# Shorter pauses in batch 0's MLP chain, and the second pass begun with row 40 of the first, in a one-core attention and MLP backward kernel

## The chip, the cores and the metric

The kernel runs on one core of one Trainium2 chip. The metric is device time in microseconds (us) for one execution; lower is better. The kernel before takes 885.9 us, the median of three runs (885.33 to 886.79).

## What is computed

A decode-time transformer block (one query token, two batches), forward and backward. The forward part is a layer norm, attention of 32 heads over a cache of 4096 keys and values, an output projection with residual, then a second layer norm and a ReLU MLP with residual:

```python
def _A_ref(x, k_cache, v_cache, wq, wo):           # B=2, Sq=1, D=640, H=32, Sk=4096, Dh=128
    q = (x @ wq)...                                 # per head
    scores = einsum("bhqd,bhkd->bhqk", q, k) * Dh**-0.5
    p = softmax(scores)
    o = einsum("bhqk,bhkd->bhqd", p, v)
    return o... @ wo
h  = x + _A_ref(_layernorm(x), k_cache, v_cache, wq, wo)
h2 = h + relu(_layernorm(h) @ w1) @ w2              # Dff = 1728
```

The outputs are `h2` and, for a given `grad_out`, the gradients of `x`, both caches, `wq`, `wo`, `w1` and `w2`. The two cache gradients are as large as the caches: 64 heads in all (2 batches x 32), each with a K and a V tile of 1 MB to read and two tiles of 1 MB to write. Both are outer products: `gV[h] = p x go` and `gK[h] = ds x q`, where `go` (the gradient of the head's output) hangs on the whole forward pass of its batch and on the MLP's backward pass.

## The kernel before

**Two passes over 64 heads.** The first pass (`p1_iter`) has rows i = 0 to 65. Row i loads and transposes K of head i, forms its scores (`s_ps`), finishes the softmax of head i-1 (`nb` L533, `ep` L540, then the weighted keys `pk` in two halves at L486), and multiplies with V of head i-2 (`m_ps`, L476, and `u_ps`, L514). The second pass (`p2_iter`, index j = 0 to 64) makes the gradients: it reads V a second time as a W tile (not for the six last heads of each batch, whose V tiles are kept), forms `dp_ps`, and writes `gV` (j) and `gK` (j-1).

**Rows and steps.** Each row is recorded in eight steps, k = 0 to 7: the points at which `p1_iter` yields. The order of instructions on each engine is the order in which this Python code issues them (a manual schedule); every engine works its own list in order and waits at semaphores. Behind each step the outer loop (from L1244 on) pumps the load queue and lets background generators run for as much as a credit allows (`bg_step`, rates in `RATES`).

**Pauses.** A generator that has issued work for one engine and will next issue work for another that needs its result yields through `wait(n)`: it goes on n steps later, so that other instructions stand between the two in the engines' lists. `spread[0]` is 1 here, and 2 once the mixed stage has begun.

**The middle of batch 0.** When row 33 has been issued, `middle_gen(0)` starts. In row 34 it closes the attention output and calls `ln_fwd` (L232): `ssum` on DVE, a column sum on PE (`colsum`, L226), mean and variance, a second column sum, an inverse square root in a few tiny DVE operations (L257 to L282) that end in `x2c`. Then 70 `hf` matmuls (L799) on PE, the ReLU and its mask on DVE (L803 to L809), a pause, and fifteen DVE products against `w1` (L697, `ttr`), in three groups; each group needs a row `fbc` that PE spreads (`bcb_ps`, L661) and ACT copies (L663). `turn()` lets at most five such products into one row of this stretch, two in step 1 and one each in steps 3, 4 and 6. The backward layer norm and the products against `wo` of the first heads follow. Only when `go_group` has marked ("go", 0, 26) may j = 0 be issued.

**Which rows hold the second pass.** `P2_AT = H + 2 + M0_ITERS` is the first row with a j (H = 32). From there every second row has one; rows 64 and 65 both do, and from then on the second pass runs alone. Up to `P2_AT` the rows from 34 on leave six of the 32 columns of `pk` to ACT (L494); behind it only two rows do. Also in rows before `P2_AT` POOL copies the column and the probabilities (L502, L580), later ACT and DVE (L504, L580).

**Loads and stores.** A list `queue` is made ahead from the same plan: K of row i, V of row i-2, and a W tile one row ahead of its j. SP issues them in this order, each as soon as one of 13 buffers of 1 MB is free. Buffers come free when `pk`'s second half is done (K) or a row's last `m_ps` (V); six hold the kept V tiles of batch 0 until j = 5. In row `P2_AT - 1` one K buffer goes over to the gradients. In the mixed stage POOL issues the stores; in the second pass alone SP does.

Of the kernel before, what the change touches and what calls it, by code (L numbers as in the profile page):

```python
# [15 lines left out]
def kernel(  # L16
# [41 lines left out]
    def f_kc(c):  # L58
        return 128 if c < NFF else F_rem
# [92 lines left out]
    def wait(n):  # L152

        end = step[0] + n * spread[0]
        while step[0] < end and not forced[0]:
            yield 0.0
        yield
# [34 lines left out]
    x2c = cols.tile([128, ND, B], BF16)  # L192
    rstd2 = cols.tile([128, B], FP32)
# [29 lines left out]
    def colsum(src, n):  # L223

        t = pst([128, 16], FP32, "mid", "csum")
        nc.tensor.matmul(t[:, 0:n], lhsT=ones_f32, rhs=src, start=True, stop=True)  # L226
        return t

    def bc(ap, n):
        return ap[:, :, None].to_broadcast([128, ap.shape[1], n])  # L230

    def ln_fwd(xs, nb, xh, rstd):  # L232

        def st(name, dt=FP32):
            return small.tile([128, nb], dt, tag=f"ln_{name}{nb}", bufs=1, name=f"ln_{name}")
        ssum = st("ssum")
        nc.vector.reduce_sum(out=ssum[:], in_=xs, axis=AX.X)
        yield from wait(2)
        t1 = colsum(ssum[:], nb)
        yield  # L240
        mean = st("mean")
        nc.vector.tensor_scalar(out=mean[:], in0=t1[:, 0:nb], scalar1=1.0 / D, scalar2=None, op0=ALU.mult)
        cent = small.tile([128, nb, ND], FP32, tag=f"ln_cent{nb}", bufs=1, name="ln_cent")
        nc.vector.tensor_tensor(out=cent[:], in0=xs, in1=bc(mean[:], ND), op=ALU.subtract)
        sq = small.tile([128, nb, ND], FP32, tag=f"ln_sq{nb}", bufs=1, name="ln_sq")
        nc.vector.tensor_tensor(out=sq[:], in0=cent[:], in1=cent[:], op=ALU.mult)
        vs = st("vs")
        nc.vector.reduce_sum(out=vs[:], in_=sq[:], axis=AX.X)
        mean_bf = st("meanb", BF16)
        nc.vector.tensor_copy(out=mean_bf[:], in_=mean[:])  # L250
        y_bf = small.tile([128, nb, ND], BF16, tag=f"ln_y{nb}", bufs=1, name="ln_y")
        nc.vector.tensor_tensor(out=y_bf[:], in0=xs, in1=bc(mean_bf[:], ND), op=ALU.subtract)
        yield from wait(2)
        t2 = colsum(vs[:], nb)
        yield from wait(1)
        var_bf = st("varb", BF16)
        nc.vector.tensor_scalar(out=var_bf[:], in0=t2[:, 0:nb], scalar1=1.0 / D, scalar2=None, op0=ALU.mult)  # L257
        z_bf = st("zb", BF16)
        nc.vector.tensor_scalar(out=z_bf[:], in0=var_bf[:], scalar1=EPS, scalar2=None, op0=ALU.add)
        z = st("z")  # L260
        nc.vector.tensor_copy(out=z[:], in_=z_bf[:])
        y = st("r")
        yi = y[:].bitcast(mybir.dt.int32)
        nc.vector.tensor_scalar(out=yi, in0=z[:].bitcast(mybir.dt.int32), scalar1=1, scalar2=None,
                                op0=ALU.logical_shift_right)
        nc.vector.tensor_scalar(out=yi, in0=yi, scalar1=-1.0, scalar2=float(0x5f3759df), op0=ALU.mult, op1=ALU.add)
        yield from wait(1)
        while at_k[0] in (0, 7) and not forced[0]:
            yield 0.0
        t = st("t")  # L270
        for c3 in (-3.0, -12.0, -768.0):
            if nb == 1:
                nc.vector.scalar_tensor_tensor(out=t[:], in0=y[:], scalar=z[:, 0:1], in1=y[:],
                                               op0=ALU.mult, op1=ALU.mult)
            else:
                nc.vector.tensor_tensor(out=t[:], in0=y[:], in1=y[:], op=ALU.mult)
                nc.vector.tensor_tensor(out=t[:], in0=t[:], in1=z[:], op=ALU.mult)
            nc.vector.scalar_tensor_tensor(out=y[:], in0=t[:], scalar=c3, in1=y[:], op0=ALU.add, op1=ALU.mult)
        ba = st("ba", BF16)
        nc.vector.scalar_tensor_tensor(out=ba[:], in0=y[:], scalar=-1.0 / 8192, in1=z[:], op0=ALU.mult, op1=ALU.mult)  # L280
        nc.vector.reciprocal(out=rstd, in_=ba[:])
        nc.vector.tensor_tensor(out=xh.rearrange("p c b -> p b c"), in0=y_bf[:], in1=bc(rstd, ND), op=ALU.mult)  # L282
        yield from wait(3)

    def ln_bwd(gh, xh, rstd, add, dst, nb):

# [484 lines left out]
    def middle_gen(b):  # L771
        if o_next[0] < (b + 1) * H // OG:
            o_group()
        u4[0] = wide_row("u")[:, 0:256].bitcast(FP32)
        nc.vector.tensor_reduce(out=u4[0], in_=u_bank[0][:].rearrange("p (s d) -> p d s", s=4),
                                axis=AX.X, op=ALU.add)
        yield
        while a_next[0] < (b + 1) * H // OG:
            if a_next[0] == o_next[0]:
                o_group()  # L780
                yield
                yield
            a_group()
            yield
        at_bf = small.tile([128, ND], BF16, tag="at_bf", bufs=1, name="at_bf")
        nc.vector.tensor_copy(out=at_bf[:], in_=asum[:, b, :])
        nc.vector.tensor_tensor(out=h1c[:, :, b], in0=xg32[:, b, :], in1=at_bf[:], op=ALU.add)
        h32 = small.tile([128, 1, ND], FP32, tag="h32", bufs=1, name="h32")
        nc.vector.tensor_copy(out=h32[:, 0, :], in_=h1c[:, :, b])
        yield ("a", b)  # L790
        u_out(b)
        yield from ln_fwd(h32[:], 1, x2c[:, :, b:b + 1], rstd2[:, b:b + 1])
        wide = 32
        hf_w = pst([128, NF, wide], FP32, "mid", "hf_ps")
        hf_ps = hf_w[:, :, 0]
        for cf in range(NF):
            kc = f_kc(cf)
            for c in range(ND):
                nc.tensor.matmul(hf_w[0:kc, cf, :], lhsT=w1_t[:, c, cf * 128:cf * 128 + kc],  # L799
                                 rhs=x2c[:, c, b:b + 1].to_broadcast([128, wide]),  # L800
                                 start=(c == 0), stop=(c == ND - 1))
            yield 0.25
        nc.vector.tensor_scalar(out=acol[:, 0:NFF, b], in0=hf_ps[:, 0:NFF], scalar1=0.0, scalar2=None, op0=ALU.max)  # L803
        if F_rem:
            nc.vector.tensor_scalar(out=acol[0:F_rem, NFF, b:b + 1], in0=hf_ps[0:F_rem, NFF:NF],
                                    scalar1=0.0, scalar2=None, op0=ALU.max)
        mask = small.tile([128, NF], FP32, tag="mask", bufs=1, name="mask")
        nc.vector.tensor_single_scalar(out=mask[:], in_=acol[:, :, b], scalar=0.0, op=ALU.is_gt)
        nc.vector.tensor_tensor(out=ghfc[:, :, b], in0=ga[:, b, :], in1=mask[:], op=ALU.mult)  # L809
        yield from wait(3)  # L810
        fbc = wide_row("fbc")
        gx2 = small.tile([128, 1, ND], FP32, tag="gx2", bufs=1, name="gx2")
        gx2p = small.tile([128, ND, 3], FP32, tag="gx2p", bufs=1, name="gx2p")
        first_f = 0
        for k, n in enumerate((ND, ND, NF - 2 * ND)):
            row = fbc[:, (k % 2) * D:(k % 2 + 1) * D]
            w = spread_some(one(ghfc, b), k * ND, n, f_kc, row)
            yield
            for c in range(ND):
                yield from turn()  # L820
                part = w1_t[:, c, first_f:first_f + w]
                ttr(part, row[:, 0:w], gx2p[:, c, k:k + 1], w, part if b else later_heads())
                yield 0.85
            first_f += w
        nc.vector.reduce_sum(out=gx2[:, 0, :], in_=gx2p[:], axis=AX.X)
        yield ("w1", b)
        yield from ln_bwd(gx2[:], x2c[:, :, b:b + 1], rstd2[:, b:b + 1], gc[:, :, b:b + 1], gh1c[:, :, b:b + 1], 1)
        row = wide_row("hbc")
        hbc, junk = row[:, 0:D], row[:, D:2 * D]
        spread_some(one(gh1c, b), 0, ND, lambda c: 128, hbc)  # L830
        yield
        yield ("gh1", b)

        first = H - KEPT[b]
        bounds = [(first, first + 2), (first + 2, H)] if b == 0 else [(first, H)]
        bounds += [(h, min(first, h + GH)) for h in range(0, first, GH)]
        for h0, h1 in bounds:
            yield from go_group(b, h0, h1, hbc, junk)
        if b > 0:
            yield from mlp_out()  # L840
# [335 lines left out]
        forced[0] = False  # L1176

    EARLY = 2
    M0_ITERS = 7
    P2_AT = H + 2 + M0_ITERS  # L1180
    RATES = (0.2, 0.8, 0.2, 0.8, 0.45)
    RATE2 = 0.65
# [180 lines left out]
```

## Time and profile before

| what | value |
|---|---|
| median of three timed runs | 885.9 us |
| the profiled execution | 883.67 us, of which the profile's span is 881.9 us |
| mean granted TensorE clock | 0.784 |
| busy share PE, DVE, ACT, POOL | 83%, 77%, 56%, 20% |
| HBM | 211.11 MB read, 149.13 MB written, 408 GB/s over the span |
| loads K, V, W | 64, 64 and 52 of 1024 KB, 15 to 19 us from issue to landing |
| first pass alone (rows 0 to 40) | up to about 252 us |
| both passes (rows 41 to 65) | about 252 to 460 us |
| second pass alone, weight gradients, end | about 460 to 882 us |

The profile is of one execution. Its page cuts the span into 40 slices of 22 us and gives for each the busy share of the engines in tenths, the granted clock, the share of time that the 16 DMA engines were busy, and the GB/s they moved. Other views cut out any stretch, or list an engine's instructions in order of time with their start, duration and, in brackets, the idle time ahead of them and what ended it. A matmul's end is modelled, so starts are the better guide on PE.

### The profile page before, as it was taken

To read this page: it belongs to the slowest core of one execution; us is meant where nothing else is said; L and a number is where in the kernel's file an instruction comes from. 1 tells how busy PE (TensorE), PEld (TensorE's weight loads), DVE (VectorE), ACT (ScalarE), POOL (GpSimd) and SP (SyncE) were. 2 spreads that over 40 slices of the span, in tenths; PEclk is the share of its full clock that TensorE was granted. 3 is DMA by queue.
4 is the path that set the end of the run, shared out by engine and by line. 5 is a ranking of instruction groups with operands and counts; after the bars stand their busy time and mean duration, and the time that the engine had idled before them with its cause. 6 is when DMAs were issued, how large, how long until landed. Compare 5 with 4: busy or idle time off the path is not lost.

```text
span 881.9 us, 24851 instructions
## 1 busy us (share of the span) xinstructions
PE 730.4 (83%) x10143; PEld 609.8 (69%) x10143; DVE 680.9 (77%) x1281; ACT 497.9 (56%) x1292; POOL 172.7 (20%) x291
## 2 busy tenths in 40 slices
PE   4999989999998998987958677778867898957880
PEld 4888878888887887876848566656646666644550
DVE  2666978867888896966878898778787789889770
ACT  1344434445777664554536878777646766636560
POOL 1344433443311000000022100211001012201110
PEclk9999999999999999988985756556556756555555
DMA  9999999999989999999999999999999999999995
GB/s 379 425 419 422 417 416 412 422 417 422 369 302 415 424 423 425 423 424 425 408 396 396 409 426 426 424 425 425 424 425 421 424 424 422 426 425 425 424 422 231
DMA packets 56034, 361.86 MB, mean 410 GB/s; under 512 B 5680, under 2 KB 11504, under 8 KB 15216
## 3 DMA queue, kind: packets, MB, share of 16 engines
q1 hardware_dynamic: 46968, 303.29, 82.9%
q0 software_dynamic: 8912, 56.97, 15.6%
q8 instruction: 80, 1.31, 0.5%
q14 instruction: 34, 0.28, 0.1%
q10 hardware_dynamic: 40, 0.01, 0.0%
HBM read 211.11 MB, written 149.13 MB: 408 GB/s over the span
## 4 chain that ended last, share of the span: by engine, by line
PE 35%; DMA 34%; DVE 16%; ACT 8%; issue 4%; SPq 0%; DVEq 0%; POOL 0%; ACTq 0%; POOLq 0%
DMA Vt<-in_A_v_cache_dram 16%; PE t_ps L440 15%; DMA out_dram<-gV 9%; PE m_ps L476 8%; DMA out_dram<-gK 5%; DVE gK L866 4%; DVE gV L866 3%; DMA Wt<-in_A_v_cache_dram 3%; PE s_ps L453 3%; ACT t_sb L445 3%; ACT gV L956 3%; DVE pk L486 2%; PE u_ps L514 2%; DVE gxj L697 2%; PE dp_ps L453 2%
## 5 line engine op out<-in xcount | busy, mean ns | idle before, releaser
L445 ACT COPY t_sb<-t_ps 128x512 f32<-128x512 f32 x479 | 273.5, 588 | 188.8 <-PE t_ps L440 185.2
L453 PEld LDWEIGHTS <-t_sb 128*128 128x128 bf16 x4096 | 177.0, 102 | 60.3 <-ACT t_sb L445 34.3
L440 PE MATMUL t_ps<-ident_f,Wt 128*128 128x128 f32 x832 | 195.0, 384 | 1.0 <-ACT t_sb L445 1.0
L476 PE MATMUL m_ps<-pk,Vt 128*128 128x129 bf16 x2048 | 171.2, 222 | 17.1 <-DMA Vt<-in_A_v_cache_dram 15.9
L486 DVE TENSOR_TENSOR pk<-Kt,ep 128x2048 bf16<-128x2048 bf16 (+1 forms) x128 | 152.7, 1193 | 42.1 <-ACT ep L540 26.2
L866 DVE TENSOR_TENSOR gK<-rb,gsp 128x2048 bf16<-128x2048 bf16 x128 | 153.0, 1224 | 22.2 <-DMA out_dram<-gV 19.3
L476 PEld LDWEIGHTS <-Vt 128*128 128x128 bf16 x2048 | 124.8, 99 | 47.8 <-issue 28.7
L440 PE MATMUL t_ps<-ident_f,Kt 128*128 128x128 f32 x1024 | 154.7, 284 | 3.5 <-DMA Kt<-in_A_k_cache_dram 3.1
L866 DVE TENSOR_TENSOR gV<-rb,pp 128x2048 bf16<-128x2048 bf16 (+1 forms) x128 | 143.2, 1144 | 17.7 <-DMA out_dram<-gV 12.2
L440 PEld LDWEIGHTS t_ps<-ident_f,Wt 128*128 128x128 f32 x832 | 135.8, 199 | 28.3 <-issue 20.9
L440 PEld LDWEIGHTS t_ps<-ident_f,Kt 128*128 128x128 f32 x1024 | 113.1, 144 | 6.0 <-ACT t_sb L445 2.3
L502 POOL COPY pk<-ep 128x16 bf16<-128x16 bf16 x80 | 83.5, 1045 | 155.2 <-ACT ep L540 75.3
L453 PE MATMUL dp_ps<-gom,t_sb 128*128 128x2 bf16 x2048 | 95.3, 168 | 22.1 <-ACT t_sb L445 21.6
L453 PE MATMUL s_ps<-qm,t_sb 128*128 128x2 bf16 x2048 | 87.3, 164 | 1.2 <-DVE t_sb L443 1.2
L1010 ACT CAST ot<-o_ps 128x512 bf16<-128x512 f32 (+3 forms) x152 | 67.3, 491 | 10.2 <-PE o_ps L1004 8.8
L604 ACT CAST MT<-m_ps 128x128 bf16<-128x128 f32 x64 | 17.0, 266 | 94.0 <-PE m_ps L476 93.9
L911 POOL COPY pp<-P_bf 128x64 bf16<-128x64 bf16 x64 | 37.1, 581 | 133.3 <-DVE gV L866 132.0
L909 ACT ACTIVATE rb<-dp_ps,rt 128x256 bf16<-128x256 f32 x64 | 30.3, 473 | 44.2 <-PE dp_ps L904 44.2
L697 DVE CUSTOM_DVE_ANT_0 hbc<-wo_t,hbc 128x640 bf16<-128x640 bf16 x64 | 52.9, 826 | 0.3
L697 DVE CUSTOM_DVE_ANT_0 gxj<-wqs,gqr 128x1024 bf16<-128x1024 bf16 x40 | 48.8, 1220 | 0.2
L956 ACT ACTIVATE gV<-rb,pa 128x128 bf16<-128x128 bf16 x152 | 46.5, 393 | 1.0 <-DMA Wt<-in_A_v_cache_dram 0.9
L1013 POOL DMA_DIRECT2D out_dram<-ot x19 | 11.0, 579 | 153.6 <-ACT ot L1010 101.1
(208 smaller groups left out, 733.4 us busy)
## 6 DMA issues: line engine op xcount, KB each, us to landing
Kt<-in_A_k_cache_dram SPq DMA_DIRECT2D x64, 1024.0 KB, 18.7
Vt<-in_A_v_cache_dram SPq DMA_DIRECT2D x64, 1024.0 KB, 15.5
Wt<-in_A_v_cache_dram SPq DMA_DIRECT2D x52, 1024.0 KB, 17.4
out_dram<-gK SPq DMA_DIRECT2D x48, 1024.0 KB, 17.8
out_dram<-gV SPq DMA_DIRECT2D x47, 1024.0 KB, 18.1
out_dram<-gV POOLq DMA_DIRECT2D x17, 1024.0 KB, 9.8
out_dram<-gK POOLq DMA_DIRECT2D x16, 1024.0 KB, 10.2
wq_t<-in_A_wq_dram SPq DMA_DIRECT2D x5, 1024.0 KB, 6.8
```

Source lines behind the costliest of these rows:

```text
L440: nc.tensor.transpose(t_ps[:, j, :], natf[:, 2 * cc:2 * cc + 2, :].rearrange("p c k -> p (c k)"), ident_f[:])
L445: nc.scalar.copy(out=t_sb[:], in_=t_ps[:])
L453: nc.tensor.matmul(dst[:, sc:sc + 2], lhsT=v[:, j, :, par], rhs=vecs[:, par, :], start=(par == 0), stop=(par == 1))
L476: nc.tensor.matmul(r["m"][:, 0:129], lhsT=r["V"][:, sc, :], rhs=r["pk"][sc // HALF][:, sc % HALF, 0:129], start=(sc == 0), stop=(sc == NSC ...
L486: nc.vector.tensor_tensor(out=p["pk"][k][:, 0:n, 0:128].rearrange("p s (a two) -> p s a two", two=2), in0=p["K"][:, sl, :].rearrange("p s ...
L502: nc.gpsimd.tensor_copy(out=col, in_=e)
L697: nc.vector.tensor_tensor_reduce(out=junk[0:kc, 0:width], in0=in0, in1=in1, scale=1.0, scalar=0.0, op0=ALU.mult, op1=ALU.add, accum_out=acc)
L866: nc.vector.tensor_tensor(out=pairs_view(dst[:, sl, :]), in0=row.rearrange("p (a two) -> p a two", two=2)[:, None, :, :].to_broadcast([128 ...
L909: nc.scalar.activation(out=rb[:], in_=bank[:, 128:384], func=ACT.Copy, scale=rt[:, b, h:h + 1])
L911: nc.gpsimd.tensor_copy(out=pp[:], in_=P_bf[:, b * H + h, :, None].to_broadcast([128, NSC, 2]))
L956: nc.scalar.activation(out=gV[:, NSC - act + k, :], in_=c["rb"][:, 0:128], func=ACT.Copy, scale=pa[:, k:k + 1])
L1010: nc.scalar.copy(out=ot[0:P, k, n0:n0 + nn], in_=o_ps[0:P, 0:nn])
```

## The change

Four pauses are cut for batch 0 alone (`less` is 1 - b, and the ReLU's pause depends on b), and `M0_ITERS` goes from 7 to 6, so `P2_AT` from 41 to 40. Nothing that is computed changes, nor any operation's shape.

```diff
-    def ln_fwd(xs, nb, xh, rstd):
+    def ln_fwd(xs, nb, xh, rstd, less=0):
...
         nc.vector.reduce_sum(out=ssum[:], in_=xs, axis=AX.X)
-        yield from wait(2)
+        yield from wait(2 - less)
         t1 = colsum(ssum[:], nb)
...
-        yield from wait(2)
+        yield from wait(2 - less)
         t2 = colsum(vs[:], nb)
...
         nc.vector.tensor_tensor(out=xh.rearrange("p c b -> p b c"), in0=y_bf[:], in1=bc(rstd, ND), op=ALU.mult)
-        yield from wait(3)
+        yield from wait(3 - less)
...
-        yield from ln_fwd(h32[:], 1, x2c[:, :, b:b + 1], rstd2[:, b:b + 1])
+        yield from ln_fwd(h32[:], 1, x2c[:, :, b:b + 1], rstd2[:, b:b + 1], 1 - b)
...
         nc.vector.tensor_tensor(out=ghfc[:, :, b], in0=ga[:, b, :], in1=mask[:], op=ALU.mult)
-        yield from wait(3)
+        yield from wait(3 if b else 1)
...
-    M0_ITERS = 7
+    M0_ITERS = 6
```

What it does to the order: the inverse square root moves from row 35, step 1, to row 34, step 6; the `hf` matmuls from row 35, steps 4 to 7, to row 35, steps 0 to 3; the first L697 product from row 36, step 3, to row 35, step 4; the mark of the first heads from row 40, step 5, to row 39, step 6. The second pass's j = 0 to 11 come one row earlier each, j = 12 and 13 stay in rows 64 and 65, and row 63 then has none. In the load order each of the first W tiles stands one row earlier.

## The prediction

> **What bounds the kernel now.** I read the page's 40 slices first. The DMA and GB/s rows are the ones to follow:
>
> ```profile
> DMA  9999999999989999999999999999999999999995
> GB/s 379 425 419 422 417 416 412 422 417 422 369 302 415 424 423 425 423 424 425 408 396 396 409 426 426 424 425 425 424 425 421 424 424 422 426 425 425 424 422 231
> ```
>
> Nearly everywhere the DMA engines are full at about 424 GB/s. The clear hole before the last slice is slices 11 and 12, 220 to 264 us. Next the busy time by stretch, cut around that hole and in the long mixed stage behind it (columns: us, busy of PE, PEld, DVE, ACT, POOL, granted clock, DMA share, GB/s):
>
> ```profile
> 220.00:230.00 10.00, 9.49 (x167) 8.58 (x167) 6.57 (x20) 6.99 (x20) 2.87 (x4) 1.00 0.90 364
> 250.00:260.00 10.00, 9.64 (x162) 8.68 (x160) 8.91 (x21) 6.36 (x19) 1.14 (x4) 1.00 0.60 239
> 300.00:350.00 50.00, 45.82 (x782) 40.40 (x780) 40.98 (x87) 29.25 (x79) 3.92 (x9) 0.97 1.01 424
> ```
>
> So the kernel is a row of bytes at 424 GB/s, plus holes. What a change in the hole is worth is how much DMA time the hole swallows, before against after. Rows of the first pass can be timed by their L533 reduction (`nb`). The one at 208.86 us is row 34's: the layer norm's first casts (L786), issued in step 1 of row 34, stand right behind it. From the time-ordered list of DVE:
>
> ```profile
> 208.86 0.29 DVE L533 TENSOR_REDUCE nb<-s_ps 128x1 f32<-128x128 f32 x1
> ...
> 213.72 0.15 DVE L257 TENSOR_SCALAR ln_varb<-csum 128x1 bf16<-128x1 f32 x1
> ...
> 214.60 0.29 DVE L533 TENSOR_REDUCE nb<-s_ps 128x1 f32<-128x128 f32 x1
> 214.81 0.21 DVE L273 SCALAR_TENSOR_TENSOR ln_t<-ln_r,ln_z 128x1 f32<-128x1 f32 x1
> ...
> 216.54 0.17 DVE L282 TENSOR_TENSOR x2c<-ln_y,rstd 128x5 bf16<-128x5 bf16 x1
> ...
> 222.40 0.29 DVE L533 TENSOR_REDUCE nb<-s_ps 128x1 f32<-128x128 f32 x1 [0.43 <-PE s_ps L531]
> ...
> 228.93 0.29 DVE L533 TENSOR_REDUCE nb<-s_ps 128x1 f32<-128x128 f32 x1
> ...
> 253.21 0.29 DVE L533 TENSOR_REDUCE nb<-s_ps 128x1 f32<-128x128 f32 x1
> ```
>
> The other four L533 are those of rows 35 (214.60), 36, 37 and 41. Rows 34 to 40 take 253.21 - 208.86 = 44.35 us, 6.3 us each. Their loads need less: one K and one V tile, 2 x 1024 KB = 2.10 MB, at 424 GB/s 4.95 us. Here compute sets the pace, and loads wait for buffers that compute frees. DMA stays full until 226 us on what was queued, then starves. Two engines take turns as the limit: PE while the `hf` matmuls run (rows 34 and 35), DVE from 226 us, where five L697 products (0.82 us each) stand in one row.
>
> **The change part by part.** The mixed stage runs j = 0 to 11 on every second row, then 12 and 13 on rows 64 and 65, in both versions. After the change j = 0 to 11 come one row earlier, and row 63 is without one. Bytes, instructions and the program behind row 65 are the same. So only two things count: when the second pass starts, and how much has been loaded by then. It starts after six compute-bound rows, not seven. The dropped row's 2.10 MB are loaded later, in the DMA-bound stage, for 4.95 us. Thus the span changes by (new start - 253.21) + 4.95, where a "start" is the `nb` of the row that holds j = 0. To break even the new start must be at 248.26. The shorter pauses must make that possible: all of batch 0's layer norm, `hf`, 15 products, backward norm and first score heads must now fit in six rows.
>
> *Rows 34 and 35.* In the changed program's instruction order the first 30 `hf` matmuls stand behind row 35's first eight transposes, ahead of L531; before, they stood late in row 35. PE has this, from its time-ordered list:
>
> ```profile
> 213.44 1.07 PE L440 MATMUL t_ps<-ident_f,Kt 128*128 128x128 f32 x8
> 214.34 0.22 PE L531 MATMUL s_ps<-neg_ident,rmax 128*128 128x128 bf16 x1
> ...
> 218.01 0.92 PE L799 MATMUL hf_ps<-x2c,w_t 128*128 128x32 bf16 x30
> ```
>
> PE would reach `hf` at 214.34, but it needs `x2c`. The two column sums move up by 1 us at most and find their inputs ready. The half product `pk` in row 34 still starts at 212.18 (a buffer frees then, L476), and ends at 213.3. Then come the five operations from L257 (213.72 to 214.60, 0.88 us), now ahead of `rmax`, then `rmax`, 0.1, then the nine from L273 to L282 (214.81 to 216.71, 1.90 us), now ahead of `nb`. So `x2c` is done at 213.3 + 0.9 + 0.1 + 1.9 = 216.3 (0.1 for rounding of overlaps). PE waits 216.3 - 214.3 = 2.0 us; behind it, in order, stand L531 and all of row 35. First term: 2.0. Its bounds: 0 (if `pk` and the small operations pack tighter and the sums come a full step early) to 2.4.
>
> Then `hf` takes 0.77 (30 matmuls, 218.01 to 218.78 before), L531 goes at 217.1 and `nb` at 217.3. The rest of the row cost PE 222.14 - 214.34 - 0.77 = 7.0 us before, and five `bcb` transposes join it (0.3): PE reaches row 36's L531 at about 224.2. That needs `rmax`, which on DVE now stands behind the first product and the second `pk` half. The first product waits for `fbc` on ACT, and ACT has the six L494 activations ahead of that copy, where before it had not:
>
> ```profile
> 224.53 0.70 ACT L663 COPY fbc<-bcb_ps 128x640 bf16<-128x640 bf16 x1
> ...
> 225.92 1.86 ACT L494 ACTIVATE pk<-Kt,pe 128x128 bf16<-128x128 bf16 x6
> ```
>
> Before, the last four transposes of a row ended 2.25 us behind L531 (214.34 to 216.59); with 35 `hf` matmuls among them (half of the 0.77 + 0.82 + 0.72 us that all 70 took) now at 217.1 + 2.25 + 1.15 = 220.5. Then on ACT the copy (0.59), the six (1.86) and `fbc` (0.70), less 0.2 of overlap: 223.4. On DVE the product (0.82), `pk` (1.23) and `rmax`: 225.6. PE waits 225.6 - 224.2 = 1.4. Bounds: 0 (if PE is itself that late) to 2.3. One more product stands ahead of `nb`, so row 36's `nb` comes at 226.5.
>
> *Rows 36 to 39.* They hold what rows 37 to 40 held, 253.21 - 228.93 = 24.28 us, and one product more (13 behind `nb`, not 12). It is a narrow one, 0.62, and DVE idled 0.88 in row 39, so I add 0.2; the bounds are 0 and 0.8. Row 40, the new start, comes at 226.5 + 24.3 + 0.2 = 251.0. The second pass begins 2.2 us earlier, where 4.95 are needed.
>
> *The start of the mixed stage* has its own hole: 0.60 at 250 to 260 us, because one K buffer goes over to the gradients and the next load waits. The same buffers change hands one row earlier; I cost it at nothing. The cover is that DMA is full afterwards; if the first pair's heads come late (they are ready in step 6 of the row ahead, before in step 5) up to 0.5 more is lost.
>
> *The end of the first pass* runs at 391 GB/s (440 to 450 us), with DMA still full. One gradient store of 1.05 MB leaves that crowd: 1.05/391 - 1.05/424 = 0.2 us won; five such stores would be 1.0, the upper bound of that gain. One more row copies its column on ACT (2 x 0.26) and its probabilities on DVE (0.17), no longer on POOL, and one row fewer has the six L494 (1.86): all of it in rows that DMA paces. On SP each W load moves past one K and V pair, the same bytes in another order.
>
> *Sum:* (251.0 - 253.21) + 4.95 - 0.2 = +2.5 us. The profiled span 881.9 becomes 884.4; the median of the timed runs, 885.9, lies 4.0 above that span, so 888.4.
>
> **The rivals.**
> 1. *The waits are covered* (faster). If neither wait opens, the dropped row gives back its whole length, row 36's 228.93 - 222.40 = 6.53, against 4.95: -1.6, with the end of the pass -1.8, 884.1. For it: DVE was idle for nearly 4 us between 218 and 226, so there is room. Against: the room lies behind `hf`, and `hf` now stands ahead of its own input.
> 2. *Only one of the two opens*, about 2 us less than forecast: 886.4. For it: the second wait hangs on ACT's order and on PE being early, both estimates.
> 3. *The clock falls* (slower still). PE waits twice within 10 us. After a long wait PE had this:
>
> ```profile
> 409.00:413.00 4.00, 1.73 (x25) 1.45 (x22) 3.72 (x9) 1.32 (x4) 0.77 (x2) 0.94 1.01 422
> 413.00:417.00 4.00, 1.22 (x11) 1.22 (x12) 0.00 (x0) 0.08 (x1) 0.00 (x0) 0.50 1.01 428
> ```
>
> A granted clock of 0.50. At half clock for one row of 5.3 us PE loses 2.7 us in a stretch that it paces: 891.1. Against: from 280 to 284 us PE was busy for 2.19 of 4 us and kept 1.00. The Trainium skill, "TensorE: Matmul & The Clock Gate", section "What's actually happening", lets the clock fall after an idle window of about 3.4 us. By that rule this rival has no price, since my waits are 2.0 and 1.4; the two stretches above agree with it.
> 4. *The change does nothing of what it says*: a forced wait for the first heads would put j = 0 back behind unfinished work. The changed order excludes it: `GQc` of heads 26 and 27 stands ahead of j = 0's first product on DVE. No chance.
>
> **How the numbers follow.** Forecast 888.4 with 0.50; covered 884.1 with 0.20; one wait 886.4 with 0.18; clock 891.1 with 0.12. About 0.2%, 1.8 us, is what a measurement of this kernel can tell from no change: 884.1 and 887.7 are the edges. The forecast's own range, 887.0 to 889.9, comes from the bounds of the two waits and of rows 36 to 39, not all at one end. Slower: nine tenths of the forecast and the clock, 0.57. Faster: six tenths of "covered", 0.12. Same: the rest, 0.31. The range 884.0 to 891.0 leaves out half of "covered" and of the clock, 0.16.
>
> **What would show it.** Right: PE idle of about 2 us ahead of the first L799, released by DVE L282; a second idle ahead of L531 in the next row, released by L592; the six-row stage lasting about 42 us from `nb` to `nb`, at any rate over 39.4 (44.35 - 4.95); the DMA share falling before 226 us. Each step is wrong if its wait is under 0.5 us. All of it is wrong if the stage lasts about 37.8 us, or if the mixed stage runs under DMA share 0.98, since then the 4.95 us are not owed.

## The result, and the profile after

The change makes the kernel slower: 888.82 us (median of 8 runs, 887.51 to 890.25) against 886.27 us (8 runs, 885.33 to 889.81), a ratio of 1.0027 with a 95% interval of 1.0015 to 1.0039, that is 1.3 to 3.5 us. The profiled execution took 888.75 us, its span is 886.9. That of before, 883.67, was below every one of its timed runs: the two spans differ by 5.0, the medians by 2.6. Below, stretches of the two traces are compared with each other; verdicts come from the timed runs.

From the page after, the two rows that were shown of before:

```profile
DMA  9999999999689999999999999999999999999995
GB/s 377 424 420 421 417 416 413 422 418 419 263 309 408 423 423 425 424 424 426 421 408 410 415 426 420 425 426 425 425 425 410 425 424 419 421 426 424 425 421 229
```

The hole is still there and has become deeper where it begins: 263 GB/s in slice 11, where before had 369. Nowhere else is there a new one. By stretch (columns as before: us, busy of PE, PEld, DVE, ACT, POOL, granted clock, DMA share, GB/s):

```profile
210.00:220.00 10.00, 6.46 (x119) 5.63 (x116) 5.25 (x24) 4.60 (x14) 2.05 (x3) 0.83 1.02 422
220.00:230.00 10.00, 8.50 (x147) 7.50 (x146) 4.74 (x13) 5.08 (x15) 1.33 (x4) 0.83 0.46 183
250.00:260.00 10.00, 9.75 (x168) 8.71 (x165) 9.75 (x25) 7.20 (x21) 1.63 (x4) 1.00 0.65 261
430.00:500.00 70.00, 56.57 (x843) 49.88 (x841) 56.78 (x114) 42.78 (x115) 12.39 (x29) 0.80 1.01 411
```

From 210 to 230 us all three compute engines stand still for a good part, at a clock of 0.83; half of the DMA time from 220 to 230 is lost (0.46, before 0.90). The last line shows the other side: 411 GB/s where the first pass ends, before 398:

```profile
430.00:500.00 70.00, 50.71 (x766) 44.91 (x763) 55.00 (x110) 42.26 (x112) 13.59 (x29) 0.79 1.00 398
```

What stands still, and for whom, is in PE's time-ordered list:

```profile
213.49 1.07 PE L440 MATMUL t_ps<-ident_f,Kt 128*128 128x128 f32 x8
218.10 0.98 PE L799 MATMUL hf_ps<-x2c,w_t 128*128 128x32 bf16 x30 [3.54 <-DMA w_t<-in_B_w_dram]
218.92 0.27 PE L531 MATMUL s_ps<-neg_ident,rmax 128*128 128x128 bf16 x1
...
226.23 1.07 PE L440 MATMUL t_ps<-ident_f,Kt 128*128 128x128 f32 x8
228.80 0.23 PE L531 MATMUL s_ps<-neg_ident,rmax 128*128 128x128 bf16 x1 [1.50 <-DVE rmax L592]
```

and in DVE's:

```profile
216.06 0.17 DVE L282 TENSOR_TENSOR x2c<-ln_y,rstd 128x5 bf16<-128x5 bf16 x1
219.23 0.29 DVE L533 TENSOR_REDUCE nb<-s_ps 128x1 f32<-128x128 f32 x1 [3.00 <-PE s_ps L531]
...
226.67 0.82 DVE L697 CUSTOM_DVE_ANT_0 P_bf<-w_t,fbc 128x640 bf16<-128x640 bf16 x1 [2.09 <-ACT fbc L663]
...
228.56 0.19 DVE L592 TENSOR_REDUCE rmax<-s_ps 128x1 bf16<-128x32 f32 x1
...
229.40 0.28 DVE L533 TENSOR_REDUCE nb<-s_ps 128x1 f32<-128x128 f32 x1
...
254.43 0.29 DVE L533 TENSOR_REDUCE nb<-s_ps 128x1 f32<-128x128 f32 x1
```

Both waits are there. The second is as forecast: 1.50 us ahead of row 36's L531, whose `rmax` stands behind the first product and behind `fbc`. The first is longer (3.54 us, not 2.0) and has another cause: `x2c` was done at 216.23, as forecast (216.3), but the `hf` matmuls also need `w1`, and its load landed at 218.1. Row 36's `nb` is at 229.40 (forecast 226.5), the new start at 254.43 (forecast 251.0): the second pass, begun a row earlier, starts 1.2 us later than before. Rows 34 to 39 took 254.43 - 208.80 = 45.6 us, more than the seven rows before (44.35).

### The profile page after: what moved, and what is told of

It is laid out like the page before. It is cut to its first block, busy times and chain, and to the rows that moved or that the text cites. A ratio compares the mean times of both kernels' runs of the same rounds, so it can differ in the third digit from the quotient of the medians.

```text
span 886.9 us, 24838 instructions
## 1 busy us (share of the span) xinstructions
PE 741.0 (84%) x10143; PEld 618.5 (70%) x10143; DVE 680.7 (77%) x1282; ACT 496.9 (56%) x1288; POOL 167.4 (19%) x287
## 4 chain that ended last, share of the span: by engine, by line
DMA 35%; PE 33%; DVE 17%; ACT 7%; issue 4%; SPq 0%; DVEq 0%; ACTq 0%; POOL 0%; POOLq 0%
PE t_ps L440 14%; DMA Vt<-in_A_v_cache_dram 12%; DMA out_dram<-gV 12%; PE m_ps L476 8%; DVE gK L866 5%; DMA out_dram<-gK 4%; DVE pk L486 3%; DVE gV L866 3%; DMA Wt<-in_A_v_cache_dram 3%; PE s_ps L453 3%; ACT gV L956 3%; DMA w_t<-in_B_w_dram 2%; PE u_ps L514 2%; ACT t_sb L445 2%; PE dp_ps L453 2%
## 5 line engine op out<-in xcount | busy, mean ns | idle before, releaser
L453 PEld LDWEIGHTS <-t_sb 128*128 128x128 bf16 x4096 | 179.2, 103 | 60.4 <-ACT t_sb L445 33.0
L440 PE MATMUL t_ps<-ident_f,Wt 128*128 128x128 f32 x832 | 197.6, 387 | 0.9 <-ACT t_sb L445 0.9
L440 PEld LDWEIGHTS t_ps<-ident_f,Wt 128*128 128x128 f32 x832 | 137.8, 201 | 28.7 <-issue 21.6
L911 POOL COPY pp<-P_bf 128x64 bf16<-128x64 bf16 x64 | 33.9, 533 | 130.9 <-DVE gV L866 128.5
L697 DVE CUSTOM_DVE_ANT_0 hbc<-wo_t,hbc 128x640 bf16<-128x640 bf16 x64 | 53.0, 828 | 0.7 <-ACT hbc L663 0.4
L697 DVE CUSTOM_DVE_ANT_0 gxj<-wqs,gqr 128x1024 bf16<-128x1024 bf16 x40 | 48.8, 1221 | 0.2
L440 PE MATMUL t_ps<-ident_f,Vt 128*128 128x128 f32 x192 | 40.9, 354 | 1.6 <-ACT t_sb L445 1.6
```

What stands on the lines that cost most here:

```text
L440: nc.tensor.transpose(t_ps[:, j, :], natf[:, 2 * cc:2 * cc + 2, :].rearrange("p c k -> p (c k)"), ident_f[:])
L453: nc.tensor.matmul(dst[:, sc:sc + 2], lhsT=v[:, j, :, par], rhs=vecs[:, par, :], start=(par == 0), stop=(par == 1))
L697: nc.vector.tensor_tensor_reduce(out=junk[0:kc, 0:width], in0=in0, in1=in1, scale=1.0, scalar=0.0, op0=ALU.mult, op1=ALU.add, accum_out=acc)
L911: nc.gpsimd.tensor_copy(out=pp[:], in_=P_bf[:, b * H + h, :, None].to_broadcast([128, NSC, 2]))
```

## The experiments

All are timed against the kernel before on the same chip. "Start" is the L533 of the row with j = 0; before, 253.21. "Waits" are PE's idle times in the trace that another engine or a load ended, from row 34's L533 to the start: 0.8 us before, 6.0 in the changed kernel. Each trace is of one execution; before, e4 and e9, which are the same up to row 41, have their starts within 0.12 us of each other (253.21, 253.31, 253.19).

**Is it the landing of `w1`?** The load is queued two rows sooner, once in the changed kernel (e1) and once in the kernel before (e2):

```diff
-    W_AT = (14, 19, 25, 30, 35)
+    W_AT = (14, 19, 25, 30, 33)
```

> The changed kernel with the w1 load queued at row 33, not 35. Theory (PE's first wait is for the w1 load, which the earlier hf matmuls now meet): hf starts when x2c is done, near 216.2 and not 218.1; the wait ahead of it falls from 3.5 to about 1.7 us, the clock stays at 1.00, row 36's L531 comes 2 to 3.5 us sooner, the new start (L533 of row 40) near 251 and not 254.4, and the time falls by 2 to 3.4 us, to 885.4 to 886.8. Rival (the waits of rows 34 and 35 are hidden by full DMA queues and do not reach the end): 888.8 within 1.

> The kernel before with the w1 load queued at row 33. Theory (there hf stands so late that w1 has just landed): no change, 886.3 within 1. Rival (w1's landing paced row 35 before, too): faster by 1 us or more.

Measured: e1 892.62, ratio 1.0060 (1.0039 to 1.0082); e2 891.87, ratio 1.0045 (1.0025 to 1.0064). Both expectations failed on the time. PE's list of e1 shows why:

```profile
210.75 1.94 PE L440 MATMUL t_ps<-ident_f,Kt 128*128 128x128 f32 x8 [3.42 <-DMA Kt<-in_A_k_cache_dram]
...
223.37 0.90 PE L799 MATMUL hf_ps<-x2c,w_t 128*128 128x32 bf16 x30 [1.34 <-DVE x2c L282]
```

The local part was right: with `w1` there, `hf` waits 1.34 us for `x2c` alone. But the 2160 KB now go ahead of a K tile while DMA is full, and PE waits 3.42 us for that tile in row 34 (3.41 in e2). The granted clock then fell to 0.50, against e1's expectation that it would stay at 1.00: for 10.2 us in e1 (209.9 to 220.1) and 6.8 in e2. The second pass starts 3.6 us later than in the changed kernel in e1, and 5.5 us later than before in e2. With `w1` at row 35's place, in the kernel before, PE waits only 0.5 us for a load behind it (a V tile, at 222.87). So the load can't simply be moved: two rows sooner it delays other tiles, and the shorter pauses ask for it before it has landed. One row sooner was not tried.

**Which part of the change costs?** The pauses alone, second pass from row 41 (e3), then the ReLU's pause alone (e5) and the layer norm's three alone (e7):

```diff
 e3 (against the changed kernel)
-    M0_ITERS = 6
+    M0_ITERS = 7
 e5 (as e3, and)
-        yield from ln_fwd(h32[:], 1, x2c[:, :, b:b + 1], rstd2[:, b:b + 1], 1 - b)
+        yield from ln_fwd(h32[:], 1, x2c[:, :, b:b + 1], rstd2[:, b:b + 1])
 e7 (as e3, and)
-        yield from wait(3 if b else 1)
+        yield from wait(3)
```

> The shorter pauses alone, second pass begun with row 41 as before. Theory (the tightened chain costs PE time in rows 34 to 36, whatever the second pass does): L533 of row 41 near 260, not 253.2, and no row dropped and no gain at the end of the first pass, so 886.3 + 6 = 892, at least 890. Rival (the cost of the change lies in the earlier second pass; the pauses are hidden): 886.3 within 1.

> The kernel before with the ReLU's pause alone cut (3 steps to 1), second pass from row 41. Theory (the layer norm's pauses, which put hf ahead of w1 and x2c, bear nearly all of the cost of e3; the second wait arises only because hf is early too): hf at 218 as before, L533 of row 41 within 1.5 us of 253.2, time 886.1 within 1.5. Rival (the ReLU's pause makes the wait for rmax and bears a good part): 888.5 or more.

> The kernel before with the layer norm's three pauses alone cut, second pass from row 41. Theory: the wait ahead of hf is 3.4 us again and the clock falls to 0.50 behind it, but the first product now stands behind rmax, so there is no second wait; L533 of row 41 near 260 and the time 892 to 893.5. Rival (the ReLU's pause bears most of e3's 9 us): below 889.

Measured: e3 895.18, ratio 1.0094 (1.0067 to 1.0121); e5 892.14, 1.0062 (1.0041 to 1.0082); e7 894.00, 1.0077 (1.0053 to 1.0101). The pauses are what costs, 8.3 us by the ratio, and the earlier second pass gives back 5.9 of them (8.3 - 2.4). For e3 and e7 the theory held in sign and place: waits of 7.9 and 6.0 us, the start at 261.93 and 261.16. Both came out worse than expected (a start near 260; 892 for e3, 892 to 893.5 for e7). For e5 it fell. `hf` started without a wait and as far behind row 34's L533 as before (9.1 us), and the start was late all the same, 260.71. Of its waits, 5.9 us, 5.0 lie behind the fifteen products:

```profile
242.97 0.38 PE L226 MATMUL csum<-lb_mm,ones_f32c 128*128 128x2 f32 x2 [1.14 <-DVE lb_mm L295]
...
249.77 0.20 PE L351 MATMUL pr_ps<-goc,sel 128*128 128x2 bf16 x2 [1.83 <-DVE goc L720]
...
259.27 0.20 PE L351 MATMUL pr_ps<-goc,sel 128*128 128x4 bf16 x2 [2.01 <-DVE goc L720]
```

These are PE operations behind pauses that nobody shortened (two steps each, in the backward norm and in the head groups). The chain arrives two steps sooner, so they stand at other steps of the row. There the DVE does a product or a half of `pk` first: before, `goc` stood at 248.49, ahead of the half at 248.80; in e5 it stands behind a half of 1.22 us that starts at 248.41. So the theory "the layer norm's pauses bear nearly all of it" is replaced: a pause in steps covers a wait only at the step where it stands, and each of the shifts tried here opened waits somewhere. Each part alone costs about two thirds or more of what both cost together (5.5 and 6.8 us, against 8.3).

**Can the change be had without the two waits?** Two versions with the second pass from row 40: the layer norm's pauses as before (e6), and the last of them lengthened (e8).

```diff
 e6 (against the changed kernel)
-        yield from ln_fwd(h32[:], 1, x2c[:, :, b:b + 1], rstd2[:, b:b + 1], 1 - b)
+        yield from ln_fwd(h32[:], 1, x2c[:, :, b:b + 1], rstd2[:, b:b + 1])
 e8 (against the changed kernel)
-        yield from wait(3 - less)
+        yield from wait(3 + less)
```

> The changed kernel with the layer norm's pauses as before: the ReLU's pause cut, second pass from row 40; the last small operations of the first two heads are issued at the row's start. Theory (a start counts for its shift plus 4.95 us for the dropped row, less about 2 us for the free row 63): no wait of 3.5 us, the start (L533 of row 40) near 247.7 to 248.7, so -5.5 to -4.5 + 4.95 - 2: 883.6 to 884.6. Rival (six rows can't hold the work, whichever pause is cut; the start is late again): 888 or more.

> The changed kernel with the layer norm's last pause at 4 steps, not 2: hf moves from step 0 of row 35 to step 2, the first product from step 4 to step 6, behind rmax; the second pass still starts with row 40. Theory (PE's two waits of rows 35 and 36 set the late start): the wait for w1 falls from 3.5 to about 2 us, the clock stays at 1.00, the wait for rmax is gone, row 36's L533 comes near 224.8 and not 229.4, row 40's near 250.3 and not 254.4, and the time is 885.5 to 887.0, some 2 us below the changed kernel. Rival (compute in six rows is the limit, the waits only show where it is short): row 40's L533 within 1 us of 254.4, time 888 or more.

Measured: e6 888.37, ratio 1.0025 (1.0012 to 1.0038), start 251.62; e8 887.41, ratio 1.0018 (1.0006 to 1.0029), start 250.87. e6 has e5's waits (4.8 us in all), so its theory failed with e5's. e8 did to the trace what was expected of it:

```profile
217.93 0.92 PE L799 MATMUL hf_ps<-x2c,w_t 128*128 128x32 bf16 x30 [2.19 <-DMA w_t<-in_B_w_dram]
...
224.60 0.22 PE L531 MATMUL s_ps<-neg_ident,rmax 128*128 128x128 bf16 x1
```

The wait for `w1` is 2.19 us, the wait for `rmax` is gone, the clock stays at 1.00, and the start is 3.6 us earlier than in the changed kernel (expected 250.3, came 250.87). The median, 887.41, lies just above the expected 885.5 to 887.0; it is 1.4 us below the changed kernel's (0.8 by the ratios) and 1.2 above before's. The interval of e8 overlaps that of the changed kernel. So the trace shows that the two waits and the clock made the start late, and the times do not settle what that is worth.

**What is won at the end of the first pass?** e4 is the kernel before, start and pauses untouched, with one pair of neighbouring rows in the middle of the mixed stage, so that row 63 is free as after the change; e9 frees row 62 as well.

```diff
-    jj = j if i >= NP1 or (i >= P2_AT and (i - P2_AT) % 2 == 0) else None
 e4
+    jj = j if i >= NP1 or (i >= P2_AT and (i - P2_AT) % 2 == int(i > 47)) else None
 e9
+    jj = j if i >= NP1 or i in (41, 43, 45, 47, 48, 50, 51, 53, 55, 57, 59, 61) else None
```

> The kernel before (pauses, start in row 41), but j = 4 stands in row 48, right behind j = 3 in row 47, so that j = 4 to 11 come one row earlier and row 63 has none, as after the change. Theory (the changed kernel won back about 1 MB, 2.3 us, between 430 and 500 us because its last rows are less crowded): faster by 1 to 2.3 us, 884.0 to 885.3, with 410 to 415 GB/s from 430 to 500 us, not 398. Rival (that rate varies from run to run): 886.3 within 1.

> The kernel before with j = 3 and 4 in rows 47 and 48, and j = 5 and 6 in rows 50 and 51, so that j = 7 to 11 come two rows earlier, and rows 62 and 63 have none. Theory (crowding of stores at the end of the first pass costs DMA rate): 430 to 500 us nearer 424 than e4's 408 GB/s, time 882.5 to 884.0. Rival (the second shift only crowds rows 47 to 51): 884.3 or more.

Measured: e4 884.33 (12 runs), ratio 0.9979 (0.9965 to 0.9993), 0.6 to 3.1 us faster; it beats both kernels. e9 886.55, ratio 1.0002 (0.9988 to 1.0016), no gain. First e4's stretch, then one of e9's (before's stands with the result above):

```profile
430.00:500.00 70.00, 54.01 (x807) 47.23 (x804) 55.39 (x110) 42.61 (x115) 11.60 (x27) 0.77 1.01 408
```

```profile
450.00:460.00 10.00, 8.10 (x138) 7.05 (x136) 8.48 (x9) 5.58 (x14) 2.68 (x6) 1.00 0.85 282
```

e4 moves 408 GB/s there (410 to 415 expected), before 398. The rate varies from one kernel to the next: in 90 us around the last rows of the first pass (from 23 us ahead of the last L533) the five kernels with row 63 free had 411 to 414 GB/s, the five without 403 to 412. Their means, 412.4 and 407.6, are 0.43 MB apart, 1.0 us; e4's timed gain is 1.9 by its ratio. In e9 the stretch falls to 382 GB/s, where a rate nearer 424 was expected, and DMA is not full in it (0.85 at 450 to 460 us); from 293 to 430 us it had kept 425, so the loss is not in the crowded rows 47 to 51. That two free rows in a row leave DMA without work fits this, but was not tested by itself. Nor is it shown that stores are what lowers the rate: the second pass alone issues at least 95 of the 128 stores of the two cache gradients, and before moved 424 GB/s from 530 to 800 us.

**The ledger over all of them.** The prediction's formula is start - 253.21, plus 4.95 where a row was dropped; the free row 63 is put in at the 1.9 that e4 measured:

| kernel | waits | start | ledger | measured (ratio, interval, in us) |
|---|---|---|---|---|
| changed | 6.0 | 254.43 | +1.2 + 4.95 - 1.9 = +4.3 | +2.4 (1.3 to 3.5) |
| e1 | 7.3 | 258.06 | +4.9 + 4.95 - 1.9 = +7.9 | +5.3 (3.5 to 7.3) |
| e2 | 4.3 | 258.68 | +5.5 | +4.0 (2.2 to 5.7) |
| e3 | 7.9 | 261.93 | +8.7 | +8.3 (5.9 to 10.7) |
| e5 | 5.9 | 260.71 | +7.5 | +5.5 (3.6 to 7.3) |
| e6 | 4.8 | 251.62 | -1.6 + 4.95 - 1.9 = +1.5 | +2.2 (1.1 to 3.4) |
| e7 | 6.0 | 261.16 | +8.0 | +6.8 (4.7 to 8.9) |
| e8 | 4.2 | 250.87 | -2.3 + 4.95 - 1.9 = +0.7 | +1.6 (0.5 to 2.6) |

For e1 and e2 the waits are counted from row 33's L533, since they begin in row 34's first step. The ledger orders the kernels nearly as the times do and misses by 0.4 to 2.6 us. Three rows lie outside their interval, the changed kernel's among them, all three too high. For e5 a reason is on record: in its profiled execution row 33 was already 1.5 us late (204.09, before 202.61), ahead of anything that its edit touches; without that its ledger is +6.0.

The bytes moved test the ledger without the times. In its trace the changed kernel is 2.50 MB behind before's at 300 us, which at 424 GB/s is 5.9 us (start and dropped row: +6.2), and 1.70 MB, 4.0 us, at 600 us, behind the last rows (ledger: +4.3). So up to there the ledger agrees with these two executions to 0.3 us. The 888.75 and 883.67 us of the same two executions differ by 5.1; over eight runs each the kernels differ by 2.4. Before's trace is of a run 2.6 us below its median, so a ledger built on it need not give the difference of the medians; where the rest lies was not found. Between kernels, too, the ledger is too steep: from e8 to the changed kernel the start is 3.6 us later and the time 0.8 us longer by the ratios, from before to e2 5.5 and 4.0.

## Why the prediction came out right

The time (888.4 against 888.8) and the sign were right, and so was the main line: only the new start and the loads already done count, and six rows must end by 248.26. But that the number came out is in good part luck: the start came 3.4 us later than forecast, 1.7 of that was offset by the free last row, and 1.9 is not accounted for. Of the signs, the second idle ahead of L531, released by L592, came as named. The first came larger and with another releaser. The six rows took 45.6 us, over the 39.4 but not about 42, and the DMA share fell before 226 us (0.80 from 221 to 222). The prediction's sums have one slip: 217.1 + 7.0 + 0.3 is 224.4, not 224.2, which would make the second wait 1.2; the start hangs on DVE's side of that wait and is not touched.

1. *The bound.* Held: no new hole elsewhere, and from 293 us to the last rows of the pass each kernel of the table moves 423 to 425 GB/s.
2. *The first wait: 2.0 forecast, 3.54 measured.* The step that failed is "PE would reach `hf` at 214.34, but it needs `x2c`". It needs `w1` as well, whose load lands at 218.0 to 218.1. The row of `hf` at 218.01, which the prediction shows, names no wait. But weight loads are listed as an engine of their own (PEld), and there the trace of before had it:

```profile
218.01 0.81 PEld L799 LDWEIGHTS <-w_t 128*128 128x128 bf16 x30 [0.28 <-DMA w_t<-in_B_w_dram]
```

A wait of 0.28 us is the only sign that `hf` stood at the earliest place that this load allows. The list of matmuls alone does not show it.
3. *The clock.* Forecast as a rival of its own with a chance of 0.12; it happened inside the forecast case. The granted clock was 0.50 from 216.6 to 223.4 us; the four transposes of row 35's first group took 1.09 us, in row 34 0.63. From the start of row 35's L531 to the start of row 36's first transposes PE took 226.23 - 218.92 = 7.3 us, against 6.4 at full clock (221.21 - 214.34 = 6.87 before, less 0.77 for the 30 moved matmuls, plus 0.28 for `bcb`): some 0.9 us, not the 2.7 that the rival had. The Trainium skill, "TensorE: Matmul & The Clock Gate", section "What's actually happening", gives an idle window of about 3.4 us for that. The traces agree in that the wait of 3.54 us lost the clock and e8's of 2.19 did not. They differ in when: the mean clock of 0.79 from 216 to 217 us puts the fall at 216.6, when PE had been idle for only 2.0 us (from 214.56).

```profile
216.00:217.00 1.00, 0.00 (x0) 0.00 (x0) 0.19 (x2) 0.00 (x0) 0.00 (x0) 0.79 0.96 391
```

Nor do the prediction's own two stretches of before agree with the rule. There the clock fell at 412.5 us, and PE's list has this around it:

```profile
411.34 1.06 PE L440 MATMUL t_ps<-ident_f,Kt 128*128 128x128 f32 x8 [1.73 <-DMA Kt<-in_A_k_cache_dram]
412.24 0.22 PE L531 MATMUL s_ps<-neg_ident,rmax 128*128 128x128 bf16 x1
415.78 1.05 PE L476 MATMUL m_ps<-pk,Vt 128*128 128x129 bf16 x8 [3.32 <-DMA Vt<-in_A_v_cache_dram]
```

The clock fell as the wait of 3.32 us began, behind a wait of 1.73 us and 1.1 us of work; the wait of 1.80 us in the other stretch lost nothing. So the rule with which the prediction set this rival's price to zero for a wait of 2.0 us was no safe ground.
4. *The second wait: 1.4 forecast, 1.50 measured,* with the releaser named. Where the first product stands behind `rmax` (e7, e8) it is gone.
5. *Rows 36 to 39: 24.5 forecast, 254.43 - 229.40 = 25.0 measured.* The new start was 3.4 late against the forecast: 1.8 at the start of `hf` (218.10, forecast 216.3), 1.1 more by row 36's `nb`, of which the clock's 0.9 is the larger part, and 0.5 from here.
6. *The start of the mixed stage, costed at nothing.* Held: 0.65 of DMA time at 250 to 260 us, before 0.60.
7. *The end of the first pass: -0.2 forecast with a bound of -1.0; e4 measures -1.9 (-3.1 to -0.6).* The forecast lies outside this interval, its bound inside. The changed kernel's own trace says the same as e4: 2.50 MB behind at 300 us and 1.70 at 600, so 0.8 MB or 1.9 us regained. The price of one store at two rates was too small a model; freeing a row went with a higher rate over the whole stretch, and what lowers that rate stays open.

With the start alone corrected, the forecast's formula gives 254.43 - 253.21 + 4.95 - 0.2 = +6.0; with the end corrected too, +4.3. That the time shows +2.4 leaves 1.9 that stay open, as under the table. What the forecast did not see at all is that other pauses, further down the chain, fit only the old phase (e5, e6). In the changed kernel itself these waits came to 0.3 us.

## What to carry to other kernels

In a hand-written order a pause covers a wait only at the step where it stands: before a chain is moved, list for each operation everything that another engine or a load must have finished, also what shows no wait now, with the time at which each was ready, and for matmuls look at the weight loads too. Where compute paces a stretch of a DMA-bound kernel, the start of the next stage, plus the DMA time of what was not loaded by then, tells where a change's cost arises and puts kernels in nearly the right order; it missed the times by up to 2.6 us here, as much as the change itself. And one part of a change can pay for another: the free row 63, alone, made the kernel faster, where the whole change made it slower.

## What the runs showed of the hardware

The five PE waits of 3.2 us and more in rows 34 and 35 (changed kernel, e1, e2, e3, e7) all cost the clock, but their length did not tell when or for how long. In the changed kernel a wait of 3.54 us cost 6.8 us of half clock (216.6 to 223.4), which began 2.0 us into the wait; in e3 a wait of 3.37 us cost 3.4 us (218.75 to 222.15), which began 0.6 us after the wait had ended; in e1 3.42 us cost 10.2. In before the clock fell behind a wait of only 1.73 us, while waits of 1.80 us there and 2.19 us in e8 cost none.

At the end of the first pass (430 to 500 us of before) the DMA engines were busy nearly all the time (share 0.98 to 1.00) and still moved 382 to 417 GB/s per 10 us, not 424; a full DMA share does not mean the full rate.
